# Linear attention and two feed-forward layers on one core: a re-planned first phase, and the second layer's output tiles issued as a group

## The chip, the core and the metric

The kernel runs on one core of one Trainium2 chip. Its engines are named here as in the profile: PE is TensorE (matmuls; PEld its weight loads), DVE is VectorE, ACT is ScalarE, POOL is GpSimd, SP is SyncE, which issues most transfers; PSUM is the memory of eight banks that PE writes, SBUF the one that holds the tiles. The metric is device time in microseconds (us) of one launch, lower being better. Times are medians of several executions; the profile is one further execution.

## The reference

```python
def phi(x):                                    # x: (4, 8, 576, 64), w_phi: (64, 128)
    proj = np.einsum('bhsd,df->bhsf', x, w_phi)
    proj = proj - np.max(np.abs(proj), axis=-1, keepdims=True)
    return np.concatenate([np.exp(proj), np.exp(-proj)], axis=-1)
q_p, k_p = (phi(q), phi(k))
kv = np.einsum('bhsf,bhsd->bhfd', k_p, v); z = np.sum(k_p, axis=2)
num = np.einsum('bhsf,bhfd->bhsd', q_p, kv)
den = np.einsum('bhsf,bhf->bhs', q_p, z)[..., None] + 1e-06
x = (num / den)                                # then laid out as (2304, 512)
h = x @ w_in;  g = h - np.tanh(h);  x = g @ w_out      # w_in (512, 2048), w_out (2048, 512), float64 inputs
p = domain_probs / (domain_probs.sum(-1, keepdims=True) + 1e-09)       # (2304, 4)
for e in range(4):                             # w1 (4, 512, 1024), w2 (4, 1024, 512)
    h = np.maximum(x @ w1[e], 0.0)
    out += p[:, e:e + 1] * (h @ w2[e])
```

## The kernel before

**Precision.** Most products are done on a high and a low part of each factor: `split3` (L389) issues three matmuls, high by high, high by low, low by high. ACT copies a value into the high part, and DVE or POOL subtracts to get the low part. The weights of the first feed-forward layer come as 64-bit words; `to_f32` makes 32-bit words of them: ACT takes the absolute value (L336), POOL raises it to a floor (L337, a `tensor_scalar` with `max`), and DVE does three bit operations (L338 to L340).

**First phase.** `k_task` and `q_task` do the attention, one pair of heads at a time: 16 key tasks and 32 query tasks. A query task ends in a division: DVE gets the reciprocals (`dn`, L610) and POOL multiplies by them (`xf`, L611). When the four query tasks of a block of 288 tokens are done, `moe_block` runs that block through the first feed-forward layer in slots of 128 hidden units: `moe_slot` is the input matmul (12 matmuls) and a chain over ACT and DVE, with the low part `gl` on POOL or DVE (L263, L264), and `moe_x2` the output matmul (12 matmuls into the four banks `accs`). `hold` and `LAG` set how many slots lie between a slot's `moe_slot` and its `moe_x2`. Only 8 of 16 hidden chunks fit in SBUF; the first two blocks run only 3 and 6 of them at first and are completed later (`add_x2`), and the other 8 chunks are converted, parked in device memory, and run afterwards over blocks of 384 tokens (`staged`, `late`, `finish`). `split_pass0` then splits the first third of the result into the operands of the second layer (`x_hi`, `x_lo`, in the order `XORD`), and the next result tiles may only be loaded over them when those splits are done (`q_users`).

**The order of the first phase** is not written out: each step is added to a graph (`Issue.add`) with an engine, a duration, a due time and its buffers, and `Issue.run` plays the graph with these durations and issues, on each free engine, the ready step with the earliest due time. The durations and the constants at the head of the file (`K_PACE`, `T_SLOT`, `PARK_LEAD`, ...) therefore decide only the order in which instructions stand in each engine's queue; on the chip every engine works through its own queue in order and waits on semaphores.

**Second layer.** It is written out in a loop over `q`, three passes (768 tokens each) of 16 steps. A step is seven products of the Strassen-Winograd form (`product(1)`, 2, 6, 7, 5, 4, 3: six matmuls of 384 columns each), whose results DVE adds up out of PSUM (`plus`, L1080) and ACT and DVE turn into hidden values (`hidden`, L1076 and L1077), and, from `q` = 2, three output tiles `l2(0)` to `l2(2)` of an earlier pair of steps (`layer2`: 12 matmuls of 512 columns into one of two banks in turn, `l2b`, then one DVE instruction that adds the tile into `yacc`, L1032). `todo` holds the next step's weight preparation (DVE sums 0 to 3, L946; ACT copies 4 to 7; POOL subtractions 8 to 11, L950), `todo2` this step's output weights (ACT L963, POOL L964); `prep(...)` issues some of `todo`. In the last step of the first and of the second pass (`q` = 15 and 31, `xnew`) every product is followed by the split of the next pass's operand (`x_hi` on ACT L766, `x_lo` L770, on DVE for products 1, 6, 5, 3), and after four steps of each of those passes a subtraction of 768 columns follows (`x_diff`, L758).

Of the kernel before, what the change touches and what calls it, by code (L numbers as in the profile page):

```python
# [9 lines left out]
F32 = mybir.dt.float32  # L10
# [11 lines left out]
LAG = 2  # L22
# [24 lines left out]
class Node:  # L47
    __slots__ = ("eng", "dur", "busy", "fn", "need", "after", "at", "key", "banks", "frees", "home", "mode", "port")
# [29 lines left out]
class Issue:  # L78
# [32 lines left out]
    def run(self):  # L111
# [3 lines left out]
        mode, port = "all", 0.0  # L115
# [11 lines left out]
        while events:  # L127
# [11 lines left out]
            for e, r in ready.items():  # L139
# [8 lines left out]
                if r:  # L148
# [10 lines left out]
                    if x.port:  # L159
                        start = max(now, port)  # L160
                    if e == "PE" and x.mode != mode:
                        start, mode = now + self.SWITCH, x.mode
                    event(start + x.busy, "idle", e)
# [40 lines left out]
def attention_moe_moe_kernel(  # L204
# [64 lines left out]
    def dma(pairs, deps=(), due=0.0, bufs=(), early=0.0):  # L269
        def fn():  # L270
            for o, i in pairs:
                SP.dma_start(out=o, in_=i)  # L272

        size = sum(n_bytes(o) for o, _ in pairs)
        return add("SP", 2.2 + 0.53 * len(pairs) + size / 300e3, fn, deps, due, bufs, busy=max(0.53 * len(pairs), size / 300e3), early=early)
# [11 lines left out]
    const.tile([128, 24], F32, name="pad")  # L287
# [15 lines left out]
    ACT.activation(out=wph, in_=wphi, func=ACTF.Copy)  # L303
    DVE.tensor_tensor(out=wpl, in0=wphi, in1=f32(wph), op=ALU.subtract)
# [22 lines left out]
    def to_f32(c, part, due, early=0.0):  # L327
# [9 lines left out]
        a = add("POOL", 1.45, lambda: POOL.tensor_scalar(out=f32(t), in0=f32(t), scalar1=TINY, scalar2=None, op0=ALU.max), [a], due + 1, [tb])  # L337
# [5 lines left out]
    def split_w(src, buf, dep, s, part, due, free=()):  # L343
        wh, wl = slots[s][:, 2 * part], slots[s][:, 2 * part + 1]
        a = add("ACT", c_act(DM), lambda: ACT.activation(out=wh, in_=src, func=ACTF.Copy), [dep, *free], due, [buf])
        b = add("POOL", c_pool(DM), lambda: POOL.tensor_tensor(out=wl, in0=src, in1=f32(wh), op=ALU.subtract), [a], due + 1, [buf])
        return [a, b]

    def direct(c, s, due):
        done = []  # L350
# [7 lines left out]
    def park(c, due):  # L358
        parked[c] = []
# [470 lines left out]
    def split_pass0(due):  # L830
# [7 lines left out]
        for users in q_users:  # L838
            users.extend(split_x)
# [306 lines left out]
```

## Time and profile before

| | us |
|---|---|
| median of 3 runs (lowest, highest) | 1412.55 (1412.22, 1415.03) |
| profiled execution, device time | 1415.48 |
| its span, first to last instruction | 1413.7 |
| PE busy in the span | 1391.4 (98%) |
| DVE, ACT, POOL busy | 1089.8, 680.8, 664.9 (77%, 48%, 47%) |
| share of the chain that ended last: PE, DVE, ACT | 89%, 7%, 2% |

How to read it: a matmul's record overlaps the next one's, so "PE busy" counts an engine that is merely not empty; gaps and the distance from one start to the next say more. The device time lies 1.8 us above the span. DVE's and POOL's busy time includes the time in which an issued instruction is held up by the other engine. The first phase takes about 670 of the 1414 us, the second layer the rest.

### The profile page before, as it was taken

The page shows a single profiled execution, that of the slowest core. Times are in us where ns is not written, and L with a number is a line of the kernel's source. Part 1 is how long each engine was busy: PE and PEld are TensorE (multiplying, and loading weights), DVE is VectorE, ACT ScalarE, POOL GpSimd, SP SyncE. Part 2 cuts the span into 40 slices and gives each one's busy share as a digit, 9 for nine tenths or more (in the row PEclk, how much of TensorE's full clock was granted, in tenths as well). Part 3 has the DMA queues.
Part 4 walks back from the last instruction along what each step waited for, and adds up shares of the span by engine and source line. Part 5 has one row for each costly group of instructions (what it writes and reads, how often), then busy time and mean ns, then how long its engine had stood idle before and what let it go on. Part 6 is the DMA issues. An engine that isn't in the chain of part 4 may idle for free.

```text
span 1413.7 us, 23154 instructions
## 1 busy us (share of the span) xinstructions
PE 1391.4 (98%) x8608; PEld 1278.1 (90%) x8608; DVE 1089.8 (77%) x1917; ACT 680.8 (48%) x1543; POOL 664.9 (47%) x547
## 2 busy tenths in 40 slices
PE   8998999999999999999999999999999999999998
PEld 6788898989999999999998899889998989899997
DVE  5888987889887868667777777877777787777774
ACT  6767666667666545445333334433333343333331
POOL 2557555554333226215454445644544465455441
PEclk9999999999999999999999999999999999999999
DMA  7342323433366513202212121223121222122211
GB/s 190 103 140 88 106 80 87 150 125 103 116 212 225 183 46 111 58 23 79 75 60 75 60 75 60 92 88 120 62 73 61 74 81 99 61 75 70 65 46 45
DMA packets 130113, 132.16 MB, mean 93 GB/s; under 512 B 54352, under 2 KB 104656, under 8 KB 130000
## 3 DMA queue, kind: packets, MB, share of 16 engines
q1 hardware_dynamic: 129840, 130.61, 29.0%
q8 instruction: 68, 1.11, 0.3%
q14 instruction: 45, 0.37, 0.1%
q10 hardware_dynamic: 160, 0.07, 0.0%
HBM read 104.83 MB, written 25.82 MB: 92 GB/s over the span
## 4 chain that ended last, share of the span: by engine, by line
PE 89%; DVE 7%; ACT 2%; issue 1%; SPq 1%; DMA 1%; POOL 0%; ACTq 0%; DVEq 0%; POOLq 0%
PE bank L389 39%; PE acc L389 39%; PE bank L601 3%; PE bank L514 2%; DVE hsm L658 1%; PE bank L571 1%; PE bank L586 1%; DVE thm L660 1%; PE acc L514 1%; PE bank L466 1%; SPq L272 1%; DVE qx L574 1%; PE acc L524 0%; DVE km L472 0%; DMA qraw<-in_q_dram 0%
## 5 line engine op out<-in xcount | busy, mean ns | idle before, releaser
L1076 ACT ACTIVATE h<-xc 128x384 fp32r<-128x384 f32 x160 | 84.3, 527 | 419.1 <-DVE xc L1080 419.1
L950 POOL TENSOR_TENSOR wslot<-wtmp,wslot 128x512 fp32r<-128x512 f32 x96 | 125.0, 1304 | 272.6 <-ACT wslot L948 172.3
L389 PE MATMUL acc<-ghm,wslot 128*128 128x288 f32 (+1 forms) x896 | 231.6, 318 | 1.8 <-DVE xq L820 1.8
L389 PE MATMUL bank<-xmem,wslot 128*128 128x288 f32 (+1 forms) x1224 | 220.1, 315 | 3.0 <-DVE thm L657 1.6
L389 PEld LDWEIGHTS bank<-xmem,wslot 128*128 128x128 f32 x1224 | 188.7, 190 | 5.3 <-DVE thm L657 1.8
L389 PE MATMUL acc<-wslot,h 128*128 128x512 f32 x768 | 188.3, 392 | 0.0
L964 POOL TENSOR_TENSOR wslot<-raw,wslot 128x512 fp32r<-128x512 f32 x96 | 138.8, 1463 | 81.0 <-ACT wslot L963 81.0
L1077 DVE SCALAR_TENSOR_TENSOR h<-xc,h 128x384 fp32r<-128x384 f32 x160 | 101.9, 637 | 94.9 <-ACT h L1076 94.9
L389 PEld LDWEIGHTS acc<-wslot,h 128*128 128x128 f32 x768 | 143.2, 188 | 27.7
L389 PE MATMUL bank<-wslot,h 128*128 128x512 f32 x672 | 166.5, 392 | 0.0
L389 PEld LDWEIGHTS acc<-ghm,wslot 128*128 128x128 f32 x896 | 159.0, 188 | 2.5 <-issue 2.5
L264 POOL TENSOR_TENSOR glm<-thm,ghm 128x288 fp32r<-128x288 f32 (+1 forms) x72 | 67.7, 940 | 179.8 <-ACT ghm L661 158.3
L389 PEld LDWEIGHTS bank<-wslot,h 128*128 128x128 f32 x672 | 125.3, 188 | 24.8 <-ACT h L1076 0.4
L389 PE MATMUL acc<-glm,wslot 128*128 128x288 f32 (+1 forms) x448 | 139.6, 312 | 0.0
L950 POOL TENSOR_TENSOR wslot<-raw,wslot 128x512 fp32r<-128x512 f32 x96 | 109.1, 1155 | 24.1 <-ACT wslot L948 24.1
L660 DVE COPY_PREDICATED thm<-sqm,hsm 128x288 f32<-128x288 int32 (+1 forms) x112 | 81.7, 729 | 38.5 <-ACT sqm L659 38.3
L1080 DVE TENSOR_TENSOR xc<-bank,xc 128x384 f32<-128x384 f32 x168 | 92.4, 550 | 13.3 <-PE bank L389 13.0
L1080 DVE TENSOR_TENSOR xc<-acc,xc 128x384 f32<-128x384 f32 x168 | 92.3, 551 | 11.2 <-PE acc L389 10.3
L946 DVE TENSOR_TENSOR wtmp<-raw 128x256 f32<-128x256 f32 x96 | 95.0, 990 | 0.0
L659 ACT ACTIVATE sqm<-sqm,b_m 128x288 f32<-128x288 f32 (+1 forms) x112 | 63.7, 568 | 47.9 <-DVE hsm L658 44.7
L389 PEld LDWEIGHTS acc<-glm,wslot 128*128 128x128 f32 x448 | 84.4, 188 | 0.0
L658 DVE SCALAR_TENSOR_TENSOR hsm<-sqm,hsm 128x288 f32<-128x288 f32 (+1 forms) x112 | 83.7, 747 | 0.1
(261 smaller groups left out, 3185.2 us busy)
## 6 DMA issues: line engine op xcount, KB each, us to landing
raw<-in_moe_w_dram SPq DMA_DIRECT2D x96, 512.0 KB, 3.5
xs<-xmem SPq DMA_DIRECT2D x16, 576.0 KB, 3.3
raw<-in_moe_w_in_dram SPq DMA_DIRECT2D x16, 512.0 KB, 4.7
raw<-in_moe_w_out_dram SPq DMA_DIRECT2D x16, 512.0 KB, 4.8
x2s<-x2m SPq DMA_DIRECT2D x10, 576.0 KB, 3.1
qraw<-in_q_dram SPq DMA_DIRECT2D x32, 144.0 KB, 2.9
xmem<-xs SPq DMA_DIRECT2D x8, 576.0 KB, 4.4
out_dram<-yacc SPq DMA_DIRECT2D x18, 256.0 KB, 2.2
```

Source lines behind the costliest of these rows:

```text
L264: return add("POOL", c_pool(n), lambda: POOL.tensor_tensor(out=o, in0=a, in1=b, op=op), deps, due, bufs)
L389: PE.matmul(ps, lhsT=a, rhs=b, start=start and n == 1, stop=stop and n == 3 * len(pairs))
L514: PE.matmul(at(bk2)[64 * e:64 * e + 64, 0:256], lhsT=w, rhs=x.rearrange("p a f -> p (a f)"), start=j == 0, stop=j == 4)
L658: y3 = add("DVE", c_dve(N), lambda: DVE.scalar_tensor_tensor(out=hs.t, in0=sq.t, scalar=P0 / P1, in1=hs.t, op0=ALU.add, op1=ALU.mult), [y1 ...
L659: x3 = add("ACT", c_act(N, ptr=True), lambda: ACT.activation(out=sq.t, in_=sq.t, func=ACTF.Relu, scale=-1.0, bias=b_m[:, 0:1]), [y3], due ...
L660: y4 = add("DVE", c_dve(N), lambda: DVE.copy_predicated(out=th.t, mask=sq.t.bitcast(I32), data=hs.t), [x3, y2, y3], due + 1.4, [th, sq, hs ...
L946: steps = [("DVE", 0.36, lambda o=o, a=a, b=b, op=op: DVE.tensor_tensor(out=o, in0=a, in1=b, op=op)) for o, a, b, op in sums]
L950: steps.append(("POOL", c_pool(n), lambda h=h, l=l, src=src: POOL.tensor_tensor(out=l, in0=src, in1=f32(h), op=ALU.subtract)))
L964: steps += [("POOL", c_pool(DM), lambda c=c: POOL.tensor_tensor(out=vl[:, c], in0=r[:, c], in1=f32(vh[:, c]), op=ALU.subtract)) for c in r ...
L1076: ACT.activation(out=hh, in_=src, func=ACTF.Relu)
L1077: DVE.scalar_tensor_tensor(out=hl, in0=src, scalar=0.0, in1=f32(hh), op0=ALU.max, op1=ALU.subtract)
L1080: DVE.tensor_tensor(out=o, in0=bk, in1=a, op=ALU.add)
```

## The change

It has five parts.

1. *The planner.* A transfer's step now holds its queue for 0.7 us per transfer, and its bytes pass one after another over one shared "wire"; a VectorE step that shares a port with GpSimd waits in the plan for the GpSimd step that is running, and a GpSimd step for such a VectorE step. The constants have new values, `LAG` goes from 2 to 3, and tables (`GLS`, `GL_UP`, `GL_LATE`, `FLOOR`, `XF`, `W_LO`, `W_LATE`, `K_SUM`) name the engine of several kinds of step.
2. *Steps on another engine.* All 32 floors (before L337) and all 32 multiplications by the reciprocal (before L611) go from POOL to DVE. Of the low parts `gl`, those of the fifth block and of the completion of the first two blocks are now all on POOL; one of the two weight subtractions of a late chunk goes to DVE.
3. *First loads.* The first query and value loads are issued on ACT's queue, an ACT instruction on a constant stands before the first that needs data, and the split of `w_phi` is a planned step. The rest of the key rows is loaded without padding zeros, and its transpose has 64 rows.
4. *Operand splits.* `XORD` is now 0, 1, 3, 6, 4, 5, 2, and the two result tiles that are loaded over the first operands wait only for the splits that read them.
5. *Second layer.* `l2(0)`, `l2(1)` and `l2(2)` stand one behind the other after product 5, with the weight preparation between them.

```diff
-LAG = 2
+LAG = 3
...
-GL = ["POOL"]
-GL2 = ["DVE", "POOL"]
-W_LEAD = -4.3
-T_TASK = 9.3
+GLS = [['POOL'], ['POOL'], ['POOL'], ['POOL'], ['POOL'], ['DVE', 'POOL'], ['DVE', 'POOL'], ['DVE']]
...
+FLOOR = ["DVE"] * 16
+XF = ["DVE"] * 8
...
-                    if x.port:
-                        start = max(now, port)
+                    if x.port and e == "DVE":
+                        if pool_end > now:
+                            start = pool_end
+                        dve_span = start, start + x.busy
+                    elif x.port:
+                        if dve_span[0] <= now < dve_span[1]:
+                            start = dve_span[1]
+                        pool_end = start + x.busy
...
-                    if x.port:
-                        port = start + x.busy
+                    if x.wire:
+                        wire = max(start + x.busy + 1.2, wire) + x.dur
+                        end = wire
...
-        return add("SP", 2.2 + 0.53 * len(pairs) + size / 300e3, fn, deps, due, bufs, busy=max(0.53 * len(pairs), size / 300e3), early=early)
+                (ACT if queue == "ACT" else SP).dma_start(out=o, in_=i)
+
+        size = slow * sum(n_bytes(o) for o, _ in pairs)
+        return add(queue, size / 300e3, fn, deps, due, bufs, busy=0.7 * len(pairs), early=early, wire=True)
...
-        a = add("POOL", 1.45, lambda: POOL.tensor_scalar(out=f32(t), in0=f32(t), scalar1=TINY, scalar2=None, op0=ALU.max), [a], due + 1, [tb])
+        if FLOOR[c] == "POOL":
+            a = add("POOL", 1.45, lambda: POOL.tensor_scalar(out=f32(t), in0=f32(t), scalar1=TINY, scalar2=None, op0=ALU.max), [a], due + 1, [tb])
+        else:
+            a = add("DVE", 0.44, lambda: DVE.tensor_scalar(out=f32(t), in0=f32(t), scalar1=TINY, scalar2=None, op0=ALU.max), [a], due + 1, [tb], port=True)
...
-        ], due=t0 - 4, bufs=[vb])
+        ], due=t0 - 4, bufs=[vb], queue="ACT" if (b, p) == (0, 0) else "SP")
...
-        a = add("POOL", c_pool(384), lambda: POOL.tensor_tensor(out=xf.t.rearrange("p r e d -> p e r d"), in0=u.t[:, :, :, 0:64], in1=dn.t.unsqueeze(3).to_broadcast([QP, 2, 3, 64]), op=ALU.mult), [a1], due, [u, dn, xf])
+        x_eng = XF[j]
+        a = add(x_eng, c_pool(384) if x_eng == "POOL" else c_dve(384), lambda: {"POOL": POOL, "DVE": DVE}[x_eng].tensor_tensor(out=xf.t.rearrange("p r e d -> p e r d"), in0=u.t[:, :, :, 0:64], in1=dn.t.unsqueeze(3).to_broadcast([QP, 2, 3, 64]), op=ALU.mult), [a1], due, [u, dn, xf], port=True)
...
-    XORD = (0, 1, 4, 5, 3, 2, 6)
+    XORD = (0, 1, 3, 6, 4, 5, 2)
...
-        for users in q_users:
-            users.extend(split_x)
+        for users, ops in zip(q_users, ((0, 1), (3, 6))):
+            users.extend(x for x, o in zip(split_x, XORD) if o in ops)
...
         hidden(0, 0, cw)
-        l2(0)
         todo2[1]()
         if q:
             load_next()
         plus(cu, product(6), cp)
-        prep(0, 1, 4, 8)
         plus(cv, product(7), cu)
-        l2(1)
-        prep(5, 9)
         p5 = product(5)
         plus(cw, p5, cv)
         hidden(1, 1, cw)
         plus(cu, p5, cu)
-        prep(2, 3, 6, 10)
+        prep(0, 1, 4, 8)
+        l2(0)
+        prep(5, 9, 2, 3)
+        l2(1)
+        prep(6, 10)
+        l2(2)
+        prep(7, 11)
         plus(cv, product(4), cv)
         hidden(1, 0, cv)
-        l2(2)
-        prep(7, 11)
         plus(cu, product(3), cu)
```

The order that this makes, at two places. First, VectorE's queue in the second layer, in step 15, the last of the first pass: `xo0l`, `xo4l`, `xo3l` are the splits of the next pass's operands, `xc` the sums of products, `h` and `xe` the low parts of hidden values, `wtmp` the sums of `prep(0, 1)`, `yacc` the output tiles. Before:

```order
L770 TENSOR_TENSOR xo0l<-xq_5065,xo0h 128x768
L1080 TENSOR_TENSOR xc_7032<-acc_81,xc_7029 128x384
L1077 SCALAR_TENSOR_TENSOR xe<-xc_7032,xe 128x384
L1032 SCALAR_TENSOR_TENSOR yacc_7023<-acc_83,pr,yacc_7023 128x512
L770 TENSOR_TENSOR xo4l<-xd_7017,xo4h 128x768
L1080 TENSOR_TENSOR xc_7030<-acc_82,xc_7029 128x384
L946 TENSOR_TENSOR wtmp_135<-raw_133 128x256
L946 TENSOR_TENSOR wtmp_135<-wtmp_135,raw_133 128x256
L1080 TENSOR_TENSOR xc_7031<-bank_84,xc_7030 128x384
L1032 SCALAR_TENSOR_TENSOR yacc_7024<-bank_87,pr,yacc_7024 128x512
L770 TENSOR_TENSOR xo3l<-xq_5066,xo3h 128x768
```

Here the step's first output tile is read out of its bank (`yacc_7023`) as the fourth instruction. The same place after the change:

```order
L787 TENSOR_TENSOR xo0l<-xq_5033,xo0h 128x768
L1097 TENSOR_TENSOR xc_7030<-acc_81,xc_7027 128x384
L1094 SCALAR_TENSOR_TENSOR xe<-xc_7030,xe 128x384
L787 TENSOR_TENSOR xo4l<-xd_7015,xo4h 128x768
L1097 TENSOR_TENSOR xc_7028<-acc_82,xc_7027 128x384
L1097 TENSOR_TENSOR xc_7029<-bank_84,xc_7028 128x384
L787 TENSOR_TENSOR xo3l<-xq_5034,xo3h 128x768
L1097 TENSOR_TENSOR xc_7030<-bank_85,xc_7029 128x384
L1094 SCALAR_TENSOR_TENSOR h_7014<-xc_7030,h_7013 128x384
L1097 TENSOR_TENSOR xc_7028<-bank_85,xc_7028 128x384
L963 TENSOR_TENSOR wtmp_133<-raw_131 128x256
L963 TENSOR_TENSOR wtmp_133<-wtmp_133,raw_131 128x256
```

The first output tile (`yacc_7021`) now stands directly behind these twelve instructions; the third tile uses the bank that it clears.

Second, PE's queue at the start of the program: `kraw` and `qraw` are raw keys and queries that PE transposes (L447, L558), L514 the first large product of a key task. Before:

```order
L586 MATMUL acc_82<-ident,pq_215 96x128 x3
L447 MATMUL bank_85<-ident,kraw_183 128x128 x4
L586 MATMUL acc_81<-ident,pq_215 96x128 x3
L558 MATMUL bank_86<-ident,qraw_191 128x96 x3
L450 MATMUL acc_83<-ident,krawr_185 128x128
L558 MATMUL acc_80<-ident,qraw_190 128x96 x3
L514 MATMUL acc_82<-kp_199,vbuf_98 64x256
```

The transposes of the third query load (the second use of `qraw_190`) stand ahead of that product. After the change the second key projection (L487) and the large product (L529) follow the second pair of loads:

```order
L574 MATMUL bank_86<-ident,qraw_185 128x96 x3
L471 MATMUL bank_87<-ident,krawr_183 64x128
L487 MATMUL acc_82<-wphi,kT_186 128x128
L487 MATMUL acc_81<-wphi,kT_186 128x128
L487 MATMUL acc_82<-wphi,kT_186 128x128
L487 MATMUL acc_81<-wphi,kT_186 128x128
L487 MATMUL acc_82<-wphi,kT_186 128x128
L487 MATMUL acc_81<-wphi,kT_186 128x128
L487 MATMUL acc_82<-wphi,kT_186 128x128
L487 MATMUL acc_81<-wphi,kT_186 128x128
L529 MATMUL acc_80<-kp_194,vbuf_98 64x256
```

The third query load's transposes now come some 30 rows further on, behind the products of the first query task (L617).

## Rows read from the trace of the kernel before

**Rows 1.** Window: start:end, length; PE, PEld, DVE, ACT, POOL busy; PEclk, DMA, GB/s
```profile
20.00:140.00 120.00, 112.44 (x1005) 96.30 (x1002) 103.09 (x205) 87.16 (x226) 73.09 (x65) 0.97 0.42 126
```
**Rows 2.** Waits of PE, whole program: us in total, times, longest
```profile
PE acc L558 <- DMA qraw<-in_q_dram: 4.0, 1, 4.0
PE bank L571 <- DVE qx L574: 2.8, 1, 2.8
PE acc L450 <- DVE qm L589: 1.9, 1, 1.9
PE acc L389 <- DVE xq L820: 1.8, 1, 1.8
```
**Rows 3.** Windows with half the granted clock; columns as in rows 1
```profile
13.10:19.90 6.80, 4.69 (x23) 2.79 (x25) 1.82 (x4) 3.59 (x10) 1.15 (x1) 0.50 0.91 212
88.20:91.60 3.40, 3.40 (x20) 3.40 (x18) 2.70 (x5) 2.95 (x8) 1.49 (x2) 0.50 0.25 58
```
**Rows 4.** Timelines of SP, ACT and PE at the start: start, us, what
```profile
12.28 0.63 SPq L272 DMA_DIRECT2D qraw<-in_q_dram  x1
...
13.73 0.29 ACT L489 ACTIVATE kpr<-kdr 128x128 f32<-128x128 f32 x1
...
15.86 0.69 PE L514 MATMUL acc<-kp,vbuf 128*64 128x256 f32 x2
```
**Rows 5.** Groups by line, 20 to 140 us: count, busy us, mean ns, idle before
```profile
L337 POOL TENSOR_SCALAR wtmp<-wtmp 128x512 f32<-128x512 f32 x14 | 21.7, 1552 | 27.3 <-ACT wtmp L336 27.2
L611 POOL TENSOR_TENSOR xf<-u,dn 96x384 f32<-96x384 f32 x11 | 11.2, 1021 | 12.7 <-DVE dn L610 11.2 <-PE bank L466 1.3
L658 DVE SCALAR_TENSOR_TENSOR hsm<-sqm,hsm 128x288 f32<-128x288 f32 x7 | 12.3, 1762 | 0.1
L338 DVE TENSOR_SCALAR wtmp<-wtmp 128x512 uint32<-128x512 uint32 x11 | 6.3, 578 | 2.0 <-POOL wtmp L337 2.0
```
**Rows 6.** Timeline of DVE before PE's wait at 132 us: start, us, what
```profile
130.33 4.29 DVE L658 SCALAR_TENSOR_TENSOR hsm<-sqm,hsm 128x288 f32<-128x288 f32 x1
```
**Rows 7.** Timeline of PE near the end: start, us, what, count
```profile
1388.12 0.33 PE L389 MATMUL acc<-xo2h,wslot 128*128 128x384 f32 x1
...
1389.16 2.92 PE L389 MATMUL acc<-wslot,h 128*128 128x512 f32 x12
1391.92 0.33 PE L389 MATMUL acc<-xo6h,wslot 128*128 128x384 f32 x1
...
1392.99 2.92 PE L389 MATMUL bank<-wslot,h 128*128 128x512 f32 x12
1395.75 2.88 PE L389 MATMUL acc<-wslot,h 128*128 128x512 f32 x12
1398.47 2.88 PE L389 MATMUL bank<-wslot,h 128*128 128x512 f32 x12
```
**Rows 8.** Timeline of DVE in step 15, whose first product starts at 876.24
```profile
887.71 0.74 DVE L1032 SCALAR_TENSOR_TENSOR yacc<-bank,pr,yacc 128x512 f32<-128x512 f32 x1
...
891.39 0.55 DVE L1080 TENSOR_TENSOR xc<-bank,xc 128x384 f32<-128x384 f32 x1
```
**Rows 9.** Timeline of PE at that product
```profile
876.24 0.33 PE L389 MATMUL acc<-xo0h,wslot 128*128 128x384 f32 x1
```
**Rows 10.** Timeline of DVE in an ordinary step, and an `x_diff`
```profile
801.95 1.04 DVE L1077 SCALAR_TENSOR_TENSOR h<-xc,h 128x384 fp32r<-128x384 f32 x1 [0.59 <-ACT h L1076]
...
804.62 1.06 DVE L946 TENSOR_TENSOR wtmp<-raw 128x256 f32<-128x256 f32 x1
805.71 0.85 DVE L946 TENSOR_TENSOR wtmp<-wtmp,raw 128x256 f32<-128x256 f32 x1
...
810.16 0.56 DVE L1077 SCALAR_TENSOR_TENSOR h<-xc,h 128x384 fp32r<-128x384 f32 x1 [0.59 <-ACT h L1076]
810.64 0.55 DVE L1080 TENSOR_TENSOR xc<-bank,xc 128x384 f32<-128x384 f32 x1
...
816.45 0.95 DVE L758 TENSOR_TENSOR xd<-xq,xd 128x768 f32<-128x768 f32 x1
```

More of the change, by code (lines that the diff above doesn't have):

```diff
@@ L47 @@
 class Node:
-    __slots__ = ("eng", "dur", "busy", "fn", "need", "after", "at", "key", "banks", "frees", "home", "mode", "port")
+    __slots__ = ("eng", "dur", "busy", "fn", "need", "after", "at", "key", "banks", "frees", "home", "mode", "port", "start", "wire")
 class Bank:
@@ L267, in at, with dma @@
         return (banks + accs)[bk.index]
-    def dma(pairs, deps=(), due=0.0, bufs=(), early=0.0):
+    def dma(pairs, deps=(), due=0.0, bufs=(), early=0.0, slow=1.0, queue="SP"):
         def fn():
             for o, i in pairs:
-                SP.dma_start(out=o, in_=i)
-        size = sum(n_bytes(o) for o, _ in pairs)
-        return add("SP", 2.2 + 0.53 * len(pairs) + size / 300e3, fn, deps, due, bufs, busy=max(0.53 * len(pairs), size / 300e3), early=early)
+                (ACT if queue == "ACT" else SP).dma_start(out=o, in_=i)
+        size = slow * sum(n_bytes(o) for o, _ in pairs)
+        return add(queue, size / 300e3, fn, deps, due, bufs, busy=0.7 * len(pairs), early=early, wire=True)
     ident = const.tile([128, 128], F32, name="ident")
@@ L345, in split_w @@
         a = add("ACT", c_act(DM), lambda: ACT.activation(out=wh, in_=src, func=ACTF.Copy), [dep, *free], due, [buf])
-        b = add("POOL", c_pool(DM), lambda: POOL.tensor_tensor(out=wl, in0=src, in1=f32(wh), op=ALU.subtract), [a], due + 1, [buf])
+        b = tt((W_LO if not free else W_LATE)[part], wl, src, f32(wh), ALU.subtract, DM, [a], due + 1, [buf])
         return [a, b]
     def direct(c, s, due):
+        due += SHIFT.get(("w", c), 0.0)
         done = []
@@ L400, in attention_moe_moe_kernel @@
     kTr_r = ring(att, 1, [128, 128], F32, "kTr")
+    DVE.memset(kTr_r.tiles[0][64:128], 0.0)
+    add("ACT", 1.4, lambda: ACT.activation(out=warm, in_=b_m, func=ACTF.Copy), (), -3.9)
+    split_phi = add("ACT", 0.2, lambda: ACT.activation(out=wph, in_=wphi, func=ACTF.Copy), (), -3.8, early=4.5)
+    split_phi = add("DVE", 0.2, lambda: DVE.tensor_tensor(out=wpl, in0=wphi, in1=f32(wph), op=ALU.subtract), [split_phi], -3.8, early=4.5)
     kd_r = ring(att, 2, [128, 4, 128], F32, "kd")
@@ L864, in attention_moe_moe_kernel @@
         xt, xdone = xt_of[j]
[L865 removed]
+        moe_block(j, [(c, c) for c in range(n_first[j])], xt, xdone, t_blk[j], t_len[j] / n_first[j], GLS[j], evac, s_rings, N, LAG)
     n_attn = len(g.nodes)
@@ L871, in attention_moe_moe_kernel @@
         ld = dma([(f32(xt.t[i]), xs[j][i]) for i in range(2)], [xs_done[j]], t2 - 10, [xt])
-        moe_block(j, rest, xt, [ld], t2, T_SLOT, ["DVE", "POOL"], add_x2, s_rings, N, LAG)
+        moe_block(j, rest, xt, [ld], t2, T_SLOT, GL_UP, add_x2, s_rings, N, LAG)
         t2 += T_SLOT * len(rest)
```

75 lines of the change are left out of this document (39 added, 36 removed).

## The prediction

> **What bounds the kernel now.** I read the waits of PE first, then PE's clock by windows, then starts on PE's timeline in the second layer, and last what VectorE does there. The list of PE's waits is short: 4.0 us for a query load at the start, 2.8 and 1.9 us for VectorE within the first 140 us, 1.8 us for VectorE at 563 us [rows 2]; a few smaller ones in the first phase make some 4 us together, and the second layer has none. PE is the bound, and in the second layer it is the only one: its matmuls follow each other without a gap. Each of the four waits in the list is followed by a stretch at half the granted clock (0.50, the lower of the two levels, 1.2 GHz): 6.8 us behind the first wait, 3.4 us behind each of the others, of which one is shown [rows 3]. Work in such a stretch takes twice as long, so the stretches cost another 3.4 + 3 x 1.7 = 8.5 us. What can be had by better order in the first phase is then about 10.5 + 8.5 + 4 = 23 us, 1.6% of the run; VectorE is busy in 103 of 120 us in its worst part, 20 to 140 us [rows 1], which is why PE's waits there are for VectorE.
>
> **The start.** PE's large key product starts at 15.86 us, behind the transposes of the third query load. That load was issued at 12.28 us, as SP's eighteenth transfer, and landed at 15.2; the last value that the product itself needs, `kpr`, was ready at 14.02 [rows 4]. In the new order the third query's transposes stand behind the product, so PE can start it about 1.8 us sooner, and the second projection fills part of the gap before it. If the gap no longer lowers the clock, the 6.8 us stretch [rows 3] gives back up to 3.4 us more. Bounds: nothing (a key load or the exponentials are late instead) and -7.4 us (the 4.0 of rows 2 and the 3.4); I take -3, the 1.8 and a third of the clock.
>
> What the second queue does by itself can be weighed against a rule of the Trainium skill ("DMA: Bandwidth & Descriptors", Issuing engines are not separate DMA queues): transfers from several engines share the same 16 DMA engines, and issuing from two saves only the sequencers' issue time. By that rule the four transfers that leave SP are worth 4 x 0.63 us to what stands behind them on SP, an estimate from the issue time in rows 4; the trace has nothing against it. It would leave the term at the -1.8 us of the new order or a little above.
>
> **The rest of the first phase.** In its worst part, 20 to 140 us, POOL is busy for 73 us [rows 1], of which 14 floors and 11 multiplications are 21.7 + 11.2 = 33 us [rows 5]. They leave. On VectorE they become 14 x 0.58 (the nearest row is the shift on the same 512 columns, L338, its waits included) and about as much for a multiplication of 384 columns, 11 x 0.58: 14.5 us more, on an engine that is busy for 103 of the 120 us. Against that stands what VectorE loses in waits for POOL: L658 takes 1762 ns on average over seven instructions [rows 5], where a low part on more columns takes 0.56 us undisturbed [rows 10], so that form alone waits 7 x 1.2 = 8.4 us; with POOL's work down by 45% some 4 of these go, and as many again in other forms, an estimate. VectorE's load thus does not fall; it grows by some 6 us. What falls is latency: a floor is a step in a chain that made a weight late, the multiplication is the last step before a block's input, and one instruction of VectorE that POOL keeps out holds up the whole queue behind it: PE's wait of 2.8 us comes behind one that lasted 4.29 us [rows 6]. With `LAG` 3 a slot's chain also has one slot more before PE needs it. The waits at 84 and 132 us with their clock stretches are 1.9 + 2.8 + 3.4 = 8.1 us, the small waits some 4. I take -9. Bounds: -12 (all gone), and +10 (VectorE's extra load and new waits come onto PE's path).
>
> At 563 us PE waits 1.8 us for an addition into `xq` which cannot load its tile until all seven operands are split [rows 2]. The loads now wait for two splits each, and these are done first. Wait and clock stretch go: -1.8 - 1.7 = -3.5 us. Bounds 0 and -3.5.
>
> **The second layer: switches.** Starts on PE's timeline give a price for going from products to output tiles and back. A product behind a product lasts 1389.16 - 1388.12 = 1.04 us; the one behind an output tile 1392.99 - 1391.92 = 1.07; an output tile behind a product 1395.75 - 1392.99 = 2.76; one behind an output tile 1398.47 - 1395.75 = 2.72 [rows 7]. One switch there and back costs 0.07 us. In 46 steps there were three of them and there will be one: 46 x 2 x 0.07 = -6.4 us. Bounds are narrow, -5 and -7.
>
> **The second layer: the bank.** The third tile of a group needs the bank of the first, and VectorE must have read the first out by then. Take 0 as the start of a step's first product. Five products are 5.2 us, two tiles 2.76 + 2.72: PE wants the bank at 10.7 us. Before, two or three products stood between any two tiles, and VectorE read the first tile early.
>
> In an ordinary step I follow VectorE from the end of product 4 of the step before; PE reaches the third tile 1.04 + 10.7 = 11.7 us after that. VectorE's chain: 0.2 to start; four times a sum followed by ACT's copy and the low part (0.55 + 0.59 to the low part's start, 0.48 until the next instruction can start), one of which is held up by POOL and takes 0.48 more (1.04 instead of 0.56) [rows 10]; three single sums, 1.6; the two weight sums, 1.06 and 0.85 (both held up by POOL) [rows 10]; the read-out, 0.74 [rows 8]. That is 0.2 + 4 x 1.62 + 0.48 + 1.6 + 1.91 + 0.74 = 11.4, and some 0.15 for PE to restart. 11.6 against 11.7: it just fits. In the 8 steps that follow an `x_diff` (0.95 us [rows 10], of which about half falls into time in which VectorE would wait for POOL anyway) it does not fit, and PE waits about 0.4: +3 us.
>
> In steps 15 and 31 VectorE also splits three operands before it comes to the first tile. The rows of before show how late that is: from 876.24, the first product [rows 9], to 891.39 + 0.55, the second sum of product 5, it took 15.7 us [rows 8]. From the first split on, that stretch of the queue holds the two weight sums and two read-outs. In the new order the same instructions stand ahead of the first read-out's end, with one read-out less (0.74), and the first split can begin some 0.4 us sooner: about 14.6 us, or 15.5 if each split meets a POOL instruction. PE wants the bank at 10.7, and waits 4 to 5 us, twice. Waits of that kind lowered the clock in every case above, so 1.7 us come on top: 2 x (4.3 + 1.7) = +12 us. Bounds: without any wait for POOL VectorE needs 12 us (a start at 2.7, three splits at the 0.95 of an `x_diff` of the same size [rows 10], five sums at 0.5, two low parts with ACT's copies at 1.15, 0.8 for the weight sums, 0.74), which makes 2 x 1.3 = +2.6 with no fall of the clock; and +14.
>
> **Sum.** -3 - 9 - 3.5 - 6.4 + 3 + 12 = -6.9 us. The profiled execution took 1415.5 us, its span 1413.7 with 1.8 around it; the median of the runs is 1412.5, 2.9 lower, and the change is applied to that: 1405.6, rounded to 1406.
>
> **Rivals.**
> - *VectorE keeps up at the turns of the passes.* If POOL and VectorE meet less often than before, steps 15 and 31 lose little, and the first phase gains in full. For it: PE never waited for VectorE in the second layer. Against: the count of instructions ahead of the read-out is fixed, and their rows sum to well over 10.7 us. Sum without the 12 and the 3: -21.9, 1391. Chance 0.25.
> - *Slower: every ordinary step misses the bank.* My margin is 0.1 us, on a chain of eleven VectorE instructions. If the chain is 0.3 longer, the third tile waits in each of the other 36 steps: 36 x 0.3 = +11, and the sum is +4, 1417. It decides as soon as the read-out of the first tile ends more than 11.5 us after product 4. For it: VectorE's 0.85 and 1.06 for sums that other rows show at 0.4 are waits for POOL, and POOL's work moves later too. Against: POOL is idle before that point. Chance 0.18.
> - *The new order does not do what it plans.* VectorE's extra load makes new waits in the first 140 us, as large as those that go; start, 563 us and the second layer stay as summed: +2, 1414.5. For it: 103 of 120 us busy [rows 1]. Chance 0.13.
>
> **How the numbers follow.** The forecast has 0.44, with a range of its own of 1398 to 1413. The range over the cases reaches from the first rival's 1391 to beyond the second's 1417, and takes in most of the bounds of the first phase: 1388 to 1421. A change under 0.2%, 2.8 us, can hardly be told from none. Faster: about 0.7 of the forecast (0.31) and all of the first rival: 0.56. The same: 0.2 of the forecast, half of the third rival, some of the second: 0.17. Slower: the rest, 0.27.
>
> **What would show it.** In the profile after: no wait of PE for a query load near 11 us and the large key product starting at about 14; no wait at 560 us; in the second layer three tiles in a row at 2.76, 2.72, 2.72, a step of about 15.5 us, and two waits of PE for `yacc` of 4 to 5 us, at about the 16th and 32nd step, each with a stretch at half clock behind it. The forecast is wrong if these two waits are missing or under 2 us, if PE waits for `yacc` in most steps, or if waits of PE on VectorE before 140 us are as long as now.

## The result, and the profile after

The changed kernel takes 1434.19 us (median of 4 runs, 1432.21 to 1437.52), the kernel before 1413.51 beside it: ratio 1.0147, 95% interval 1.0126 to 1.0168. It is slower by 20.7 us; the forecast was 1406 with a range to 1421. The profiled execution took 1432.21 us, its span is 1430.4.

The two halves of the program moved in opposite directions. PE starts the second layer's first product at 649.84 us (before 658.36), and the stretch from there to the last product grew from 750.8 to 776.3 us: -8.5 and +25.6 in these two executions.

PE's waits in the changed kernel, as in [rows 2]:

```profile
PE acc L408 <- DVE yacc L1049: 10.2, 10, 4.1
PE bank L408 <- DVE yacc L1049: 4.7, 2, 2.5
PE bank L408 <- DVE yacc L1047: 3.3, 1, 3.3
PE acc L543 <- ACT kvT L556: 1.8, 2, 1.2
...
PE bank L587 <- DVE qx L590: 1.3, 1, 1.3
...
PE acc L574 <- DMA qraw<-in_q_dram: 1.0, 1, 1.0
```

The four waits of [rows 2] are gone or small. In their place PE waits 18.2 us for `yacc`, the read-out of an output tile. In the ordinary steps a yacc wait stops the weight load ahead of a matmul (by 0.29 us at the third tile shown below) and does not appear in this list. So I measured each step by the time from its first product to the next step's. Before, all steps from step 2 on take 15.64 us (15.96 and 15.95 at steps 16 and 32). After:

| steps | us each | against before, all together |
|---|---|---|
| 32 ordinary ones | 15.67 to 15.71 | +1.2 |
| 8 behind an `x_diff` | 16.05 to 16.09 | +3.4 |
| 15 and 31 (operand splits) | 21.50, 21.48 | +11.7 |
| 16 and 32 (behind them) | 19.92, 17.99 | +6.0 |
| 2 (first with output tiles) | 19.11 | +3.5 |

The last step has no next one; from its first product to the last matmul PE takes 31.64 us, before 31.77.

PE's timeline at the three tiles of step 15, and of an ordinary step (start, us, what; wait before it):

```profile
878.46 2.92 PE L408 MATMUL acc<-wslot,h 128*128 128x512 f32 x12
881.22 2.88 PE L408 MATMUL bank<-wslot,h 128*128 128x512 f32 x12
888.21 4.61 PE L408 MATMUL acc<-wslot,h 128*128 128x512 f32 x12 [4.11 <-DVE yacc L1049]
...
1299.49 0.33 PE L408 MATMUL acc<-xo6h,wslot 128*128 128x384 f32 x1
...
1305.73 2.92 PE L408 MATMUL acc<-wslot,h 128*128 128x512 f32 x12
1308.49 2.88 PE L408 MATMUL bank<-wslot,h 128*128 128x512 f32 x12
1311.24 3.02 PE L408 MATMUL acc<-wslot,h 128*128 128x512 f32 x12
```

The second tile follows the first by 2.76 us, as in [rows 7]. The third follows the second by 2.75 in the ordinary step, against 2.72 undisturbed, and then takes 3.02, against 2.88: together 0.17 late. In step 15 it follows by 6.99 and takes 4.61, at half the clock. VectorE at the same two places:

```profile
879.23 1.89 DVE L787 TENSOR_TENSOR xo4l<-xd,xo4h 128x768 fp32r<-128x768 f32 x1 [0.65 <-ACT xo4h L783]
...
885.62 1.01 DVE L963 TENSOR_TENSOR wtmp<-raw 128x256 f32<-128x256 f32 x1
886.67 0.83 DVE L963 TENSOR_TENSOR wtmp<-wtmp,raw 128x256 f32<-128x256 f32 x1
887.42 0.74 DVE L1049 SCALAR_TENSOR_TENSOR yacc<-acc,pr,yacc 128x512 f32<-128x512 f32 x1
...
1305.03 1.21 DVE L1097 TENSOR_TENSOR xc<-bank,xc 128x384 f32<-128x384 f32 x2
1306.34 0.56 DVE L1097 TENSOR_TENSOR xc<-acc,xc 128x384 f32<-128x384 f32 x1
...
1307.97 0.55 DVE L1097 TENSOR_TENSOR xc<-acc,xc 128x384 f32<-128x384 f32 x1
1308.44 1.20 DVE L963 TENSOR_TENSOR wtmp<-raw 128x256 f32<-128x256 f32 x1
1309.67 0.85 DVE L963 TENSOR_TENSOR wtmp<-wtmp,raw 128x256 f32<-128x256 f32 x1
1310.45 0.74 DVE L1049 SCALAR_TENSOR_TENSOR yacc<-acc,pr,yacc 128x512 f32<-128x512 f32 x1
1311.11 0.41 DVE L963 TENSOR_TENSOR wtmp<-raw 128x256 f32<-128x256 f32 x1
1311.44 1.51 DVE L963 TENSOR_TENSOR wtmp<-raw,wtmp 128x256 f32<-128x256 f32 x1
```

In the ordinary step the read-out ends at 1311.19. PE wants the bank at 1308.49 + 2.72 = 1311.21 and needs a moment to go on: just missed. In step 15 PE wants it at 883.94, and the read-out ends at 888.16. The two weight sums ahead of it take 1.84 us there and 2.05 in the ordinary step, where an undisturbed one takes 0.41; POOL subtractions run beside them in both. What makes step 15 later is what stands further ahead, the splits of the operands (`xo4l` takes 1.89 us).

In the first phase, the windows of [rows 1] and of the stretch around 563 us (start:end, length; PE, PEld, DVE, ACT, POOL busy; PEclk, DMA, GB/s):

```profile
20.00:140.00 120.00, 113.50 (x1050) 97.51 (x1046) 112.04 (x239) 91.69 (x237) 48.29 (x42) 1.00 0.46 134
...
460.00:640.00 180.00, 180.00 (x1039) 179.72 (x1039) 132.58 (x224) 92.21 (x188) 54.80 (x44) 1.00 0.27 80
```

POOL's load fell from 73 to 48 us, VectorE's rose from 103 to 112, and PE got 1050 matmuls into the window instead of 1005; e2 below shows that most of this difference goes with the clock. Around 563 us PE has no gap left.

### The profile page after: what moved, and what is told of

It reads as the page before. It is cut to its first block, busy times and chain, and to the rows that moved or that the text cites. A ratio compares the mean times of both kernels' runs of the same rounds, so it can differ in the third digit from the quotient of the medians.

```text
span 1430.4 us, 23263 instructions
## 1 busy us (share of the span) xinstructions
PE 1394.4 (97%) x8608; PEld 1271.8 (89%) x8608; DVE 1125.9 (79%) x1978; ACT 690.5 (48%) x1544; POOL 585.0 (41%) x483
## 4 chain that ended last, share of the span: by engine, by line
PE 76%; DVE 15%; ACT 6%; issue 2%; DMA 1%; SPq 0%; ACTq 0%; DVEq 0%
PE acc L408 34%; PE bank L408 33%; DVE xc L1097 3%; PE bank L617 2%; DVE wtmp L963 2%; ACT h L1093 2%; PE bank L529 1%; DVE h L1094 1%; PE bank L602 1%; DVE hsm L675 1%; DVE qx L590 1%; PE bank L587 1%; DVE yacc L1049 1%; PE bank L487 1%; DVE xe L1094 1%
## 5 line engine op out<-in xcount | busy, mean ns | idle before, releaser
L981 POOL TENSOR_TENSOR wslot<-raw,wslot 128x512 fp32r<-128x512 f32 x96 | 138.7, 1460 | 199.0 <-ACT wslot L980 199.0
L408 PE MATMUL acc<-wslot,h 128*128 128x512 f32 x768 | 192.9, 399 | 10.2 <-DVE yacc L1049 10.2
L280 POOL TENSOR_TENSOR glm<-thm,ghm 128x288 fp32r<-128x288 f32 (+1 forms) x80 | 81.0, 1013 | 266.1 <-ACT ghm L678 213.9
L408 PEld LDWEIGHTS acc<-wslot,h 128*128 128x128 f32 x768 | 144.3, 191 | 46.8 <-DVE yacc L1049 17.1
L965 ACT ACTIVATE wslot<-wtmp 128x512 fp32r<-128x512 f32 x96 | 60.7, 633 | 184.8 <-DVE wtmp L963 184.8
L967 POOL TENSOR_TENSOR wslot<-raw,wslot 128x512 fp32r<-128x512 f32 x96 | 104.4, 1108 | 100.7 <-ACT wslot L965 100.7
L677 DVE COPY_PREDICATED thm<-sqm,hsm 128x288 f32<-128x288 int32 (+1 forms) x112 | 76.6, 685 | 31.0 <-ACT sqm L676 30.7
L678 ACT ACTIVATE ghm<-thm 128x288 fp32r<-128x288 f32 (+1 forms) x112 | 53.9, 481 | 61.9 <-PE acc L408 38.4
```

What stands on the lines that cost most here:

```text
L280: return add("POOL", c_pool(n), lambda: POOL.tensor_tensor(out=o, in0=a, in1=b, op=op), deps, due, bufs)
L408: PE.matmul(ps, lhsT=a, rhs=b, start=start and n == 1, stop=stop and n == 3 * len(pairs))
L677: y4 = add("DVE", c_dve(N), lambda: DVE.copy_predicated(out=th.t, mask=sq.t.bitcast(I32), data=hs.t), [x3, y2, y3], due + 1.4, [th, sq, hs ...
L678: x4 = add("ACT", c_act(N), lambda: ACT.activation(out=gh.t, in_=th.t, func=ACTF.Copy), [y4], due + 2, [th, gh])
L965: steps.append(("ACT", c_act(n), lambda h=h, src=src: ACT.activation(out=h, in_=src, func=ACTF.Copy)))
L967: steps.append(("POOL", c_pool(n), lambda h=h, l=l, src=src: POOL.tensor_tensor(out=l, in0=src, in1=f32(h), op=ALU.subtract)))
```

## The experiments

Times are medians; each ratio is to the kernel before, run on the same chip beside it. "First product" is the start of the second layer in the profiled execution, "half clock" the time at 0.5 ahead of it.

| kernel | us | ratio (95%) | first product | half clock |
|---|---|---|---|---|
| before | 1413.5 | | 658.4 | 17.1 |
| after | 1434.2 | 1.0147 (1.0126, 1.0168) | 649.8 | 6.8 |
| e1 old tiles | 1409.3 | 0.9959 (0.9942, 0.9975) | 652.4 | 10.2 |
| e2 only group | 1440.9 | 1.0188 (1.0171, 1.0205) | 654.3 | 6.8 |
| e3 read first | 1412.3 | 0.9978 (0.9966, 0.9990) | 653.6 | 13.7 |
| e4 three banks | 1411.3 | 0.9980 (0.9968, 0.9992) | 650.6 | 0 |
| f1 mixed | 1409.7 | 0.9974 (0.9964, 0.9983) | 653.6 | 10.2 |
| f2 mixed, POOL | 1406.3 | 0.9947 (0.9933, 0.9961) | 649.4 | 0 |
| f3 only splits | 1418.9 | 1.0041 (1.0027, 1.0055) | 662.6 | 13.7 |
| f4 only floors | 1404.8 | 0.9937 (0.9924, 0.9949) | 647.6 | 6.8 |
| g1 floors, wide | 1399.5 | 0.9902 (0.9889, 0.9916) | 647.2 | 6.8 |
| g2 old paces | 1412.9 | 0.9991 (0.9982, 1.0000) | 656.3 | 13.7 |
| g3 floors POOL | 1415.6 | 1.0014 (1.0005, 1.0023) | 659.1 | 10.2 |
| g4 floors, queue | 1411.4 | 0.9980 (0.9971, 0.9989) | 653.3 | 3.4 |

**Which half, e1 and e2.** e1 is the changed kernel with the whole step written as before, e2 the kernel before with the step written as after:

```diff
         hidden(0, 0, cw)
+        l2(0)
...
+        l2(1)
+        prep(5, 9)
...
+        plus(cv, product(4), cv)
+        hidden(1, 0, cv)
         l2(2)
```

> The changed kernel with the three output tiles back at their old places between the products; everything else as changed. Theory (all of the loss is the grouping of the tiles): the second layer takes 750.8 us again and the first phase keeps its 8.5 us: 1404 to 1409 us, no wait of PE for yacc. Rival (the loss comes from the other parts, by the state in which the first phase leaves the second layer's first loads and splits): steps 2, 16 and 32 stay long and the time stays above 1415.

> The kernel before with nothing but the three output tiles issued one behind the other. Theory (all of the loss is the grouping): the second layer grows by 25.6 us, to 1437 to 1441 us, with the waits of PE for yacc in steps 2, 15, 16, 31 and 32. Rival (the loss needs the re-planned first phase as well): below 1425.

e1 took 1409.25 us, at the upper end of what was expected, all its steps 15.64 (15.96 and 15.97 at 16 and 32), no wait for yacc. e2 took 1440.86. The grouping alone costs 26.9 us on the old first phase (e2 against before) and 24.9 on the new one (after against e1): it is all of the loss, in either surrounding. The rest of the change is worth -4.7 us, not the -15.5 of the forecast, nor the -8.5 of two single profiles that e1's expectation took over.

e2 also has the first phase of before in a second execution. Its waits are those of [rows 2] (3.9, 2.8, 1.9, 1.7), but the half clock behind three of them is not there. The windows of [rows 1] and [rows 3]:

```profile
20.00:140.00 120.00, 111.91 (x1034) 95.94 (x1031) 104.65 (x208) 88.05 (x229) 73.46 (x65) 1.00 0.42 125
88.20:91.60 3.40, 3.40 (x36) 3.39 (x36) 3.19 (x6) 2.82 (x8) 1.85 (x3) 1.00 0.26 59
```

36 matmuls at 1.00 stand where the profile of before had 20 at 0.50, and from 20 to 140 us there are 1034 instead of 1005: 29 of the changed kernel's 45 more can be had without any change of order. The first product, at 654.3 us, is 4.1 earlier with the same order on PE. In the five profiles with the changed first phase (after, e1, e3, e4, f1) it stands at 649.8 to 653.6, so one profile fixes it to some 4 us only. Over the 62 runs of the kernel before in these comparisons, the mean granted clock goes from 0.994 (9 runs, median 1415.5 us) to 0.999 (3 runs, 1410.5): about 1 us per 0.001, so some 1.2 us for a stretch of 3.4. The stretches come and go between executions of one program, and I had read them from an execution that had many.

**What the grouped tiles wait for, e3 and e4.** e3 lets VectorE read the first tile before it makes the weight sums; e4 gives the three tiles three banks:

```diff
-        prep(0, 1, 4, 8)
         l2(0)
+        prep(0, 1, 4, 8)
         prep(5, 9, 2, 3)
```
```diff
-    l1b = banks[0:3] + accs[0:3]
-    l2b = [banks[3], accs[3]]
+    l1b = banks[0:3] + accs[0:2]
+    l2b = [banks[3], accs[3], accs[2]]
...
-        y = l2b[(n * TP + t) % 2]
+        y = l2b[(n * TP + t) % 3]
```

> The changed kernel, with the group's first tile issued ahead of the two weight sums on VectorE, so that it is read out some 2 us sooner; the three tiles still stand together in two banks. Theory (PE waits at the third tile for the first tile's bank): ordinary steps fall from 15.68 to 15.50 us, the 8 steps behind an x_diff from 16.07 to 15.50, steps 2, 15, 16, 31 and 32 lose 2 us each at most (their waits of 3.5 to 5.9 stay in part): 7 + 4.6 + about 10 us, 1412 us, range 1409 to 1417. Rival (the steps are longer because three tiles in a row cost PE itself more than the rows near the end said): ordinary steps stay at 15.68 and the time above 1420.

> The changed kernel with three banks for the output tiles and five in place of six for the products; the order of every queue as changed. Theory (the bank alone is what PE waits for): all 46 steps take 15.50 us, no wait of PE for yacc, no half clock in the second layer; the second layer is 744 us, the whole 1400 to 1405 us. Rival 1 (VectorE itself is too late at the turns, so a wait only moves to the next product's bank): steps 15 and 31 keep 2 us or more of their wait, 1406 to 1412. Rival 2 (five banks are too few for the products): new waits of PE for xc in every step, above 1412.

e3, PE and then VectorE in an ordinary step:

```profile
1289.40 2.92 PE L408 MATMUL acc<-wslot,h 128*128 128x512 f32 x12
1292.16 2.88 PE L408 MATMUL bank<-wslot,h 128*128 128x512 f32 x12
1294.88 2.88 PE L408 MATMUL acc<-wslot,h 128*128 128x512 f32 x12
```
```profile
1292.36 0.75 DVE L1049 SCALAR_TENSOR_TENSOR yacc<-acc,pr,yacc 128x512 f32<-128x512 f32 x1 [0.17 <-PE acc L408]
1293.03 0.97 DVE L963 TENSOR_TENSOR wtmp<-raw 128x256 f32<-128x256 f32 x1
1294.04 0.42 DVE L963 TENSOR_TENSOR wtmp<-wtmp,raw 128x256 f32<-128x256 f32 x1
1294.38 0.42 DVE L963 TENSOR_TENSOR wtmp<-raw 128x256 f32<-128x256 f32 x1
1294.71 0.42 DVE L963 TENSOR_TENSOR wtmp<-raw,wtmp 128x256 f32<-128x256 f32 x1
```

VectorE now waits for the tile (0.17 us), and PE's tiles follow by 2.76 and 2.72 and take 2.88: every ordinary step takes 15.51 in e3 and in e4, those behind an `x_diff` too. So the saving per switch was right, and in an ordinary step the bank was what PE waited for. At the turns of the passes the two part. e3 keeps 19.67 and 16.37 us (steps 15, 16), 19.58 and 16.06 (31, 32). e4 has 15.51 in steps 15 and 31, but 19.91 in 16 and 32, with a half-clock stretch in each. Its waits there:

```profile
PE bank L408 <- DVE xc L1097: 2.9, 2, 2.5
PE acc L408 <- DVE xc L1097: 2.5, 1, 2.5
```

With the output tiles' bank free, PE runs ahead until a product's bank is missing one step later. That is the mechanism of rival 1 of the expectation (VectorE itself is too late at a turn, whichever bank shows it), and its time; but its sign, a wait left in steps 15 and 31, did not come. e4 also has five banks for the products where e3 has six, and no run tells how much of the waits in steps 16 and 32 this makes. My reading, not tested by itself, is that the old order had room at the turns: two or three products alternate with a tile of 2.76 us, and VectorE catches up during the tile, which five products in a row do not allow.

**Old order where VectorE is behind, f1.** e3, with the step written as before if `q in (2, 15, 16, 31, 32)`.

> The changed kernel with the first tile issued ahead of the two weight sums, and in steps 2, 15, 16, 31 and 32 the output tiles at their old places. Theory (41 steps gain the switches and the other five only need the old order to let VectorE keep up): 41 x 0.13 = 5.3 us below the changed kernel with all tiles at their old places (1409.3), 1404 us, range 1400 to 1406; no wait of PE for yacc or xc in the second layer. Rival (a grouped step hands a backlog of VectorE on to the old-order steps behind it): steps 15 and 31 or their followers stay above 16.5 us and the time is 1408 or more.

It took 1409.72, no faster than e1: steps 15 and 31 are at 15.64, but 16 and 17 take 16.87 and 17.31, 32 and 33 16.84 and 17.71. The rival was right on place, but not on engine. PE's timeline in step 17:

```profile
906.22 0.44 PE L408 MATMUL bank<-xo5h,wslot 128*128 128x384 f32 x1 [0.50 <-ACT wslot L965]
...
907.57 0.61 PE L408 MATMUL bank<-xo5h,wslot 128*128 128x384 f32 x2 [0.73 <-POOL wslot L967]
```

My reading: a grouped step issues the next step's weight preparation late, and when the next step also has operand splits for ACT and POOL, the weights are not ready. e1, with the old order throughout, has no such wait, nor has g1 below, which has the old order one step ahead of these and one behind them as well.

**The floors, f2 and f4; the operand splits, f3.** f2 is f1 with `FLOOR = ["POOL"] * 16` and `XF = ["POOL"] * 8`. f4 is the kernel before with the floor (L337) and the multiplication (L611) issued on DVE, nothing else. f3 is the kernel before with the new `XORD` and `q_users`.

> As the mixed kernel, with all floors and all multiplications by the reciprocal back on GpSimd (planned so). My forecast's reasoning (their move to VectorE removes latency and is worth several us of the first phase): the first phase is 5 to 10 us longer, with waits of PE for VectorE behind long instructions back in the first 140 us: 1409 to 1414 us. Rival (the move was worth nothing, since VectorE's added load in the first 140 us gives back what GpSimd's relief brings): within 3 us of the mixed kernel, either sign.

> The kernel before with only the floors and the multiplications on VectorE, planned with the old rules and constants. My forecast's step (GpSimd's relief is what brings most of the gain of the rest of the first phase): 5 to 9 us faster than before, 1405 to 1409. Rival (VectorE's load gives it back, and what the first phase gains comes with the new plan): within 3 us of before, or slower.

> The kernel before with only the new order of the operand splits and the loads waiting for two splits each. My forecast's step: the wait at about 563 us and the half-clock stretch behind it go, 3.5 us. Rival (the half-clock stretch stands in one execution's trace and not in another's of the same order, so only the wait itself can be counted on): 1.8 us, 1411 to 1412.5 us. Either way PE's wait for xq is gone.

f4 took 1404.76: the move of the floors alone, under the old plan, brings 8.8 us, what my step said (-9). f2 took 1406.31 with a second layer as long as before's (750.8 us): the new plan without the move brings 7.3 us. It lies 3.4 us below f1, where the theory expected it above and the rival within 3 us. Both together, in e1, bring 4.7. The two parts do not add up. I looked for a cause that both cure. The form on which the step rested was L658 (L675 after), 12.3 us in seven instructions from 20 to 140 us [rows 5]. The same group in f2, then in f4:

```profile
L675 DVE SCALAR_TENSOR_TENSOR hsm<-sqm,hsm 128x288 f32<-128x288 f32 x7 | 5.7, 807 | 0.0
```
```profile
L658 DVE SCALAR_TENSOR_TENSOR hsm<-sqm,hsm 128x288 f32<-128x288 f32 x7 | 5.3, 751 | 0.1
```

Either a new order with POOL as loaded as ever, or the old order with POOL relieved, takes some 7 us off this form's busy time; the waits of 2.8 and 1.9 us are in neither. The windows from 20 to 140 us of f2, and of f4:

```profile
20.00:140.00 120.00, 116.84 (x1077) 100.38 (x1074) 104.75 (x217) 91.62 (x237) 75.46 (x67) 1.00 0.45 135
```
```profile
20.00:140.00 120.00, 116.84 (x1076) 98.68 (x1072) 110.88 (x240) 90.97 (x233) 46.80 (x43) 0.99 0.47 138
```

They get 1077 and 1076 matmuls into the window, the changed kernel 1050. But the form alone does not decide the time: in the changed kernel it takes 4.3 us for eight instructions, less than in either, and in g4 below 5.3 us, as in f4, while g4 is 6.6 us slower. Nor does VectorE's load: 110.9 us in f4 and 112.0 in the changed kernel. Why the two parts bring less together than each alone stays open.

f3 is slower than before by 5 us and missed both expectations. Its list of waits has

```profile
PE acc L389 <- ACT ghm L661: 2.4, 1, 2.4
...
PE acc L389 <- DVE xq L820: 1.2, 1, 1.2
```

The wait for xq is shorter, not gone, and a new one of 2.4 us near the end of the phase, with a half-clock stretch at 656.7, comes in. f4, without the new splits, has no wait for xq either. So this step of the change is not what removes that wait by itself; what else in the new plan makes it work there was not tried.

**More of the plan, g2 to g4, and a better kernel, g1.** g2 is e1 with `T_TASK = 9.3`, `W_LEAD = -4.3`, `K_PACE = 1.21`; g3 is e1 with the floors alone back on POOL; g4 is f4 with the first query and value loads on ACT's queue. g1 is f4 with the step of e3, and the step as before if `q in (2, 14, 15, 16, 17, 30, 31, 32, 33)`.

> The changed kernel with the tiles at their old places (1409.3 us) and with the distances of attention tasks, weight conversions and key steps as before (9.3, -4.3 and 1.21 in place of 10.8, -10.8 and 1.17); rules and tables of the planner as changed. Theory (these distances pack the first 80 us worse for a VectorE that has the floors): 1404 to 1407, PE busy above 116 of the 120 us from 20 to 140. Rival (the planner's new rules or the longer lag do it): 1408 or more.

> The changed kernel with the tiles at their old places and the floors alone back on GpSimd; the multiplications stay on VectorE. Theory (in the new plan it is the floors' load on VectorE between 50 and 80 us that holds up ACT and through it PE): 1405 to 1407, as with both moved back. Rival (it is the multiplications, the last step ahead of a block's input): 1409 or more.

> The kernel before with the floors and multiplications on VectorE (1404.8 us), and the first query and value loads on ACT's queue. My forecast's step for the start: 1.8 to 3 us less, 1402 to 1403. Rival (PE's wait for the third query load only becomes a wait for the exponentials and their copies behind it): no change, 1404 to 1406.

> The kernel before with the floors and multiplications on VectorE (1404.8 us), and in the second layer 37 steps with the tiles as a group, the first tile ahead of the weight sums; steps 2, 14 to 17 and 30 to 33 keep the old places. Theory (a grouped step issues the next step's weight preparation late, so a step with operand splits needs an old-order step ahead of it and two behind it; then nothing is lost): 37 x 0.13 = 4.8 us less, 1400 us, every grouped step 15.51, steps 16, 17, 32 and 33 at most 16.0. Rival (the backlog comes from the turns themselves, whatever stands around them): again some 3 us longer around each turn, 1404 to 1406.

The theories of g2, g3 and g4 all fell, and all to the slow side: +3.6 and +6.3 us against e1, +6.6 against f4. The rivals' bounds hold for g2 and g3, but neither of them said that it would be slower than the kernel it starts from. Each is a small edit, and each re-orders the queues of all engines. Over eight plans the first product stands anywhere from 647 to 663 us. No single load that I read from a window predicts where. g4 also bears on the start: PE's longest wait for a query load is 2.6 us, against 3.0 in f4 and 4.1 in g1, which have one first phase, and new waits come in, the longest of 1.9 us for `kTr` from VectorE. The rule of the Trainium skill ("DMA: Bandwidth & Descriptors", Issuing engines are not separate DMA queues) that the forecast weighed says that a second queue saves issue time only. Nothing here speaks against it, but no run tests it by itself, since g4 re-orders all queues.

g1 took 1399.51, 14 us below the kernel before, where 1400 was expected: f4 has 8.8 of it, and g1 takes 5.3 off f4. PE's timeline in two ordinary steps:

```profile
775.66 2.92 PE L389 MATMUL acc<-wslot,h 128*128 128x512 f32 x12
778.42 2.88 PE L389 MATMUL bank<-wslot,h 128*128 128x512 f32 x12
781.14 2.88 PE L389 MATMUL acc<-wslot,h 128*128 128x512 f32 x12
791.16 1.55 PE L389 MATMUL bank<-wslot,h 128*128 128x512 f32 x6
```

From 775.66 to 791.16 is 15.50. PE has no wait in the second layer, steps 16 and 32 take 15.97 and 15.95 as before, and the layer takes 745.8 us, 5 less than before.

## Why the prediction was wrong

Taken by its own terms.

- **Start, -3.** About -1 is seen: the wait for the query load fell from 4.0 to 1.0 us and PE did 108 matmuls in the first 20 us instead of 83, but after 40 us the lead is 277 to 269 (271 in e1 and f1, with the same order). This step failed: the large key product did not move. It now stands behind the other transposes and waits for the exponentials:

```profile
13.87 0.69 PE L574 MATMUL bank<-ident,qraw 96*128 96x96 f32 x3
...
15.92 0.65 PE L529 MATMUL acc<-kp,vbuf 128*64 128x256 f32 x2
16.83 1.52 PE L529 MATMUL acc<-kp,vbuf 128*64 128x256 f32 x12 [0.26 <-ACT kp L496]
```

  I had it at 14, with the exponentials as early as before. They are not: ACT begins them at 14.60, before at 10.98. I also counted on a third of the clock. The stretch at half clock is still there and as long, from 8.1 to 14.9. What it costs is seen between two executions of this order in which PE's wait for the query load is 1.4 us, f1 with such a stretch and e4 without. Their first 20 us, then those of the changed kernel:

```profile
0.00:20.00 20.00, 16.19 (x102) 13.04 (x104) 8.36 (x26) 9.02 (x21) 0.70 (x6) 0.83 0.55 131
```
```profile
0.00:20.00 20.00, 16.74 (x110) 13.28 (x112) 9.15 (x27) 9.10 (x21) 0.70 (x6) 1.00 0.60 141
```
```profile
0.00:20.00 20.00, 16.66 (x108) 13.40 (x110) 8.95 (x26) 9.04 (x21) 0.70 (x6) 0.83 0.58 138
```

  The large key product starts at 16.51 in f1 and at 15.78 in e4. By this pair the stretch costs some 0.7 us here, not the 3.4 that its length suggests. The changed kernel's profile makes up for part of it with a wait for the query load that is 0.4 us shorter.
- **Rest of the first phase, -9, and 563 us, -3.5.** This step failed. The floors by themselves, under the old plan, bring what I had put down for the whole term (f4, -8.8). That is luck, since the forecast was for the new plan. I took the floors and the new plan as one cause with one gain, without asking what each leaves for the other. The bounds (-12 to +10) held it; the value did not. And 3.4 + 1.7 us of it were half-clock stretches of one execution. All terms of the first phase came to -15.5; e1 measures -4.7.
- **Switches, -6.4.** The price was right (15.51 against 15.64 in the grouped steps of g1). But the changed kernel never got it, because of the next term.
- **The bank in an ordinary step, 0.** This step failed. My chain on VectorE ended at 11.6 us, PE came at 11.7. In the trace PE goes on 0.16 to 0.2 us late in every step but the five long ones and the last: 40 steps, about 7 us. The product behind product 4 starts at 1299.49 and the read-out ends at 1311.19: 11.70 us, where my chain without the restart had 11.41. Of the 0.29, the three single sums have 0.18 (1305.03 to 1306.34 for two and 1307.97 to 1308.44 for the third, 1.78 instead of 1.6), and the two weight sums 0.10 (2.01 until the read-out starts, instead of 1.91). Rival 2 named this mechanism and its deciding point, 11.5 us; it came at about half the price of 0.3 per step. "PE waits for `yacc` in most steps" was also one of the forecast's own signs of being wrong.
- **x_diff, +3.** Right in mechanism and size: 0.4 us over the other steps, 16.07 against 15.67, eight times.
- **Turns, +12.** Right: 4.11 us of wait and a half-clock stretch of 3.4 us in steps 15 and 31, +11.7 together.
- **What was missing: +9.5 us.** I closed the account at the end of steps 15 and 31. VectorE's queue was not empty then: in step 16 the read-out of the first tile ended 8.1 us after that tile began on PE, in an ordinary step 5.5, and PE waited 2.5 us more, with a half-clock stretch at 909.2; in step 32 it waited 2.2 without one. And step 2 follows two steps of seven bare products (7.28 us each), in which VectorE falls behind as well. PE's rows there:

```profile
678.53 1.66 PE L408 MATMUL bank<-wslot,xe 128*128 128x512 f32 x6 [3.28 <-DVE yacc L1047]
...
908.15 2.04 PE L408 MATMUL bank<-wslot,h 128*128 128x512 f32 x6 [2.55 <-DVE yacc L1049]
```

The sum of the second layer was +8.6; it was +25.6. The 17 us between them are the ordinary steps (some 7), steps 16 and 32 (6.0), step 2 (3.5), and small differences. The first phase was off by another 10.8 by medians (-4.7 instead of -15.5): the part of it that is neither the start nor the clock stretches stays unexplained, as does why the floors and the new plan do not add.

## What to carry to other kernels

When outputs are grouped to save switches, the spaces between them are what the reading engine used to catch up: follow its queue past the critical step until it is empty again, and through the steps with unusual work at the beginning and at each turn. A margin of 1% on a chain of eleven instructions is no margin; put the read-out that frees a bank ahead of work that nobody waits for. And two parts of a change need not add up (8.8 and 7.3 us alone, 4.7 together): ask of each what it brings when the other is already there. A stretch at half clock that one profile shows may be missing in the next execution of the same program; look at a second one before its price goes into a sum.

## What the runs showed of the hardware that I had not expected

- The half-clock stretches of the first phase belong to an execution, not to the program. The same wait of 3.3 us in step 2 is followed by full speed in the changed kernel (678.53 above, six matmuls in 1.66 us) and by half clock in e2:

```profile
683.00 2.93 PE L389 MATMUL bank<-wslot,xe 128*128 128x512 f32 x6 [3.30 <-DVE yacc L1030]
```

- The order on VectorE decides how long it is held up by GpSimd. With the read-out first, the four weight sums of a step take 0.97 + 3 x 0.42 = 2.2 us in e3; in the changed kernel's order 1.20 + 0.85 + 0.41 + 1.51 = 4.0. The long ones are those beside which POOL works: its subtractions stand at 1308.06 to 1310.23 and from 1311.33 to 1312.67 there, and at 1291.73 to 1293.72 in e3.
